# Fewer, larger backward loads, a padded copy of wo in DRAM, and filling products in four 32-column tiles

## The chip, the cores and the metric

One NeuronCore of a Trainium2 chip runs the whole program. The metric is the device time of one execution in microseconds (us); less is better. The engines are named as in the profile: PE (TensorE, matrix products; PEld its weight loads), DVE (VectorE), ACT (ScalarE), POOL (GpSimd) and SP (SyncE, which here only issues transfers). SBUF is the on-chip memory that transfers fill and empty, PSUM the memory that TensorE writes.

## The reference

A transformer block with attention and a gated feed-forward part side by side, and its gradient. 2048 tokens, width 448, 16 heads of 28, feed-forward width 1792, all in bfloat16:

```
xn  = layernorm(x)
q, k, v = split(xn @ wqkv)                      # 16 heads of 28
o   = softmax(q k^T * 28**-0.5) v
out = x + o @ wo + (silu(xn @ w_gate) * (xn @ w_up)) @ w_down
return out, gradients of (x, wqkv, wo, w_gate, w_up, w_down) for grad_out
```

Seven outputs: `out_0` is `out`, `out_1` the gradient of x, `out_2` of wqkv, `out_3` of wo, `out_4` and `out_5` of w_gate and w_up, `out_6` of w_down.

## The kernel before

Heads are taken in four groups of four (G = 4). A head's 28 columns are padded to 32 (HP), so four heads fill the 128 rows of a tile; `pv` rotates the places of the heads by two for V and dO.

**Forward half, 0 to about 611 us.** 256 slots (`slot`), one for each group, block of 512 queries and block of 128 keys, form the scores and their exponentials. Between them a list of units fills TensorE: projections, the feed-forward part with its whole backward (`a_unit`, `u_unit`, `dh_unit`, `dw_unit`), and the attention output with dO (`o_unit`, `mid1` to `mid3`). What the second half needs goes to DRAM: `QD_d` (for each group and query block: Q, dO and both transposed), `KD_d` (K, V, K transposed), `OT_d` (the attention output, transposed), `F_d` (hidden product and its two gradients), `fT_d`, `wT_d`, `wqT_d`.

The output weight wo is loaded once at the start into `wo_pad` (L249-L250): four loads of 28 rows, one for each head of a group, each to rows HP * pv(hh) of a tile that was set to zero (L184). From there DMA transposes fill `woT` (L665), the last of them at slot 13 (L703).

**Backward half, about 614 to 1404 us.** 512 steps k in the order group g, head pair hp, key block kc, query block qc, quarter qi. The loop at L1230 writes out the order of the instructions by hand. Four steps (m = k % 4) make a turn, of which there are 128:

- every step: `row(k)` issues four products in 32-row tiles, two score products of step k into `sb` (L810) and two dO V^T products of step k-1 into `db` (L818). `ew(k)` issues two exponentials on ScalarE (`e_sb`, L834) and two multiplications on VectorE (`ds_sb`, L840), and for three steps of four a DMA transpose of ds (`dst_dma`, L827) on the SP queue. Then SP issues the stores that have waited two steps (`flush`) and the loads that are due (`drop`);
- m = 1: `kv` (dV/dK, L913 and L917: four products in 32-column tiles into `acc`) for the steps that are ready, then `dq_unit` (L944: 16 products in 32-column tiles into `genb`), whose result ScalarE takes away (L948, L957) and POOL adds up (L959);
- m = 2: `kv`, then a filling unit is opened and fills for R2 = 250 ns;
- m = 3: the filling unit goes on for R3 = 750 ns (in one turn of four a `kv` that was put off comes first);
- m = 0: the unit goes on for R0 = 400 ns, the fourth quarter's ds is transposed on TensorE (`tr_unit`, L895, taken away by ScalarE at L900), and the unit is brought to its end.

`fill_step(room)` takes products from the open unit until the room is used up; each `yield` gives a product's estimated ns. With 189 ns a product, R2 takes one and R3 four.

Filling units, in order: `late_dw` (four units of 16 products, the last feed-forward weight gradients), `y_unit` (the forward output: 7 or 11 products for each of 16 token tiles and two halves), `dx_unit` (feed-forward part of the gradient of x: 10, 8 or 10 products, 48 units), `dc_unit` (attention part: 9 products, 16 units), and in between, when a group is done, `dsp_unit` and `dsq_unit` (transposes) and `dwq_unit` (four units of 16 products, gradient of wqkv). A unit's products add up in one bank, `genb`, which has a single buffer shared with `dq_unit`; at its end VectorE or ScalarE takes the bank away. `y_unit` writes `y` (two buffers), which SP stores.

**Loads of the backward half.** `drip(key, pieces, due)` puts pieces of a load into a list ordered by due step. `drop` works through it once a step, at a rate in bytes that meets the due steps (at least 100 KB a step), one SP transfer for each piece (L767). `have(key)` issues at once what is left of a load when it is needed (L773). All transfers of the second half, the transposes among them, go through SP in the order in which they are written. The loads and their pieces: `load_q` (qd, two pieces of 256 KB), `load_k` (kd, 256 and 128 KB), fT (four), wd_sb (seven), wo_sb (four loads of 28 rows from A_wo into a tile that POOL sets to zero, L1048 and L1054), `load_y` (h_c four, x_c two, o_c two for each half), `load_w` (wguT, one for each of 14 blocks), `load_dx` (dau_c, one for each of 14 blocks and four chunks).

The filling products before the change are all of this form (here `dx_unit`), with a weight of 128 columns (64 in the last of four chunks of `late_dw` and `dwq_unit`):

```
PE.matmul(ps[:, :D], lhsT=d[:, i // 2, i % 2, tsl], rhs=dxs["w", fq][:, i // 2, i % 2, :],
          start=(i == 0), stop=(i == n - 1))
```

Of the kernel before, what the change touches and what calls it, by code (L numbers as in the profile page):

```python
# [12 lines left out]
BF16 = mybir.dt.bfloat16  # L13
# [4 lines left out]
D = 448  # L18
H = 16
DH = 28  # L20
# [18 lines left out]
def pv(hh):  # L39


    return (hh + 2) % 4
# [61 lines left out]
def kernel(  # L104
# [32 lines left out]
    OT_d = dram.tile([4, P, G, 512], BF16)  # L137
    F_d = dram.tile([4, P, NFC, 3, 512], BF16)
    fT_d = dram.tile([P, 4, 2, 4, P], BF16)
    wT_d = dram.tile([P, NFC, 2, DP_], BF16)  # L140
    wqT_d = dram.tile([P, 3 * G, DP_], BF16)
    dqkvT_d = dram.tile([3 * G, P, S], BF16)
# [557 lines left out]
    for k in range(12, 16):  # L700
        slot(k)
        if k == 13:
            woT_load(3)  # L703
    qside, kside = {}, {}
    kq = None

# [67 lines left out]

    def load_q(g, qc):
        t = new_q(g, qc)
        drip(("q", g, qc), [(t[:, i:i + 2], QD_d[g, qc, :, i:i + 2]) for i in (0, 2)], 128 * g + 4 * qc - 4)

    def load_k(g, kc):
        t = new_k(g, kc)  # L780
        drip(("k", g, kc), [(t[:, 0:2], KD_d[g, kc, :, 0:2]), (t[:, 2], KD_d[g, kc, :, 2])], 128 * g + 16 * kc - 4)

    steps = [(g, hp, kc, qc, qi) for g in range(G) for hp in range(2) for kc in range(4)
             for qc in range(4) for qi in range(4)]
# [84 lines left out]
        x()  # L869
    fT = bk.tile([P, 4, 2, 4, P], BF16, name="dsp", bufs=1)  # L870
    w2 = bk.tile([P, 4, 2, P], BF16, name="dqT", bufs=1)
    drip(("f",), [(fT[:, sc], fT_d[:, sc]) for sc in range(4)], 10)

    def late_dw(c):
        d0, dn = DCH[c]
        have(("f",))
        ps = ps_g.tile([P, 2, P], FP32, name="genb")
        for t in range(NT):
            PE.matmul(ps[:dn], lhsT=xn_sp[:, t, d0:d0 + dn], rhs=fT[:, t // 4, :, t % 4, :],
                      start=(t == 0), stop=(t == NT - 1))  # L880
            if t < NT - 1:
                yield 110
        DVE.tensor_copy(out=w2[:dn, c], in_=ps[:dn])
        for a, o in enumerate((out_4, out_5)):
            store(o[d0:d0 + dn, F - P:], w2[:dn, c, a])
        yield 110

    dq_acc = bk.tile([P, S // 2], FP32, name="dq_acc", bufs=1)

    def tr_unit(b):  # L890
        for qi in (3,) if b < NB // 4 - 1 else (2, 3):
# [113 lines left out]
    def dwq_unit(g, c, tag="genb"):  # L1005
        d0, dn = DCH[c]
        ps = (ps_b if tag == "rest" else ps_g).tile([P, 3 * P], FP32, name=tag, bufs=2 if tag == "rest" else 1)
        for t in range(NT):
            PE.matmul(ps[:dn, :], lhsT=xn_sp[:, t, d0:d0 + dn], rhs=dsp[g][:, t].rearrange("p k r -> p (k r)"),
                      start=(t == 0), stop=(t == NT - 1))  # L1010
            if t < NT - 1:
                yield 162
        o = bk.tile([P, 3, 4, DH], BF16, name="dwq_o")
        p4 = ps[:].rearrange("p (k h r) -> p k h r", k=3, r=HP)
        cp = ACTE.copy if tag == "rest" else DVE.tensor_copy
        cp(out=o[:dn, 0], in_=p4[:dn, 0, :, :DH])
        cp(out=o[:dn, 1:3, 0:2, :], in_=p4[:dn, 1, :, :DH].rearrange("p (k h) r -> p k h r", k=2))
        cp(out=o[:dn, 2, 2:4, :], in_=p4[:dn, 2, 0:2, :DH])
        cp(out=o[:dn, 1, 2:4, :], in_=p4[:dn, 2, 2:4, :DH])
        store(wq_out[d0:d0 + dn, :, g * 4 * DH:(g + 1) * 4 * DH],  # L1020
              o[:dn].rearrange("p k h r -> p k (h r)"))
        s_done.add((g, c))
        yield 162
# [7 lines left out]
    def load_y(ch, half):  # L1031
        due = now + 32 if now else 36 + 16 * half
        h_c = yp.tile([P, NH, 512], BF16, name="h_c", bufs=3)
        drip(("y", ch, half), [(h_c[:, a:b], F_d[ch, :, half * NH + a:half * NH + b, 0, :])
                               for a, b in ((0, 2), (2, 4), (4, 6), (6, 7))], due)
        ych[ch, half] = h_c
        if half == 0:
            x_c = yp.tile([P, 4, D], BF16, name="x_c")
            drip(("y", ch, half), [(x_c[:, a:a + 2], x_d[:, 4 * ch + a:4 * ch + a + 2, :]) for a in (0, 2)], due)
            ych[ch, 2] = x_c  # L1040
        else:
            o_c = yp.tile([P, G, 512], BF16, name="o_c")
            drip(("y", ch, half), [(o_c[:, a:a + 2], OT_d[ch, :, a:a + 2]) for a in (0, 2)], due)
            ych[ch, 3] = o_c

    wd_sb = yp.tile([P, NFC, D], BF16, name="wd_sb", bufs=1)
    wo_sb = yp.tile([P, G, D], BF16, name="wo_sb", bufs=1)
    POOL.memset(wo_sb[:], 0.0)  # L1048
    wd_v = B_w_down.rearrange("(fc p) d -> p fc d", p=P)
    drip(("y", 0, 0), [(wd_sb[:, a:a + 2, :], wd_v[:, a:a + 2, :]) for a in (0, 2, 4, 6)], 35)  # L1050
    load_y(0, 0)
    load_k(0, 2)
    drip(("y", 0, 1), [(wd_sb[:, a:a + 2, :], wd_v[:, a:a + 2, :]) for a in (8, 10, 12)], 50)
    drip(("y", 0, 1), [(wo_sb[HP * pv(hh):HP * pv(hh) + DH, :, :], wo_v[hh]) for hh in range(4)], 50)  # L1054

    load_y(0, 1)
    load_k(0, 3)
# [1 line left out]
    def y_unit(ch, half, ti):  # L1059
        if ti == 0:  # L1060
            have(("y", ch, half))
            nxt = 2 * ch + half + 2
            if nxt < 8:
                load_y(nxt // 2, nxt % 2)
        tsl = slice(ti * P, (ti + 1) * P)
        mm = [(ych[ch, half][:, i, tsl], wd_sb[:, half * NH + i, :]) for i in range(NH)]
        if half:
            mm += [(ych[ch, 3][:, i, tsl], wo_sb[:, i, :]) for i in range(G)]
        ps = ps_g.tile([P, 512], FP32, name="genb")
        for i, (l, r) in enumerate(mm):  # L1070
            PE.matmul(ps[:, :D], lhsT=l, rhs=r, start=(i == 0), stop=(i == len(mm) - 1))
            if i < len(mm) - 1:
                yield 189
        if half == 0:
            yts[ti] = yp.tile([P, D], FP32, name="yt", bufs=5)
            DVE.tensor_tensor(out=yts[ti][:], in0=ps[:, :D], in1=ych[ch, 2][:, ti, :], op=ALU.add)
        else:
            y = yp.tile([P, D], BF16, name="y")
            DVE.tensor_tensor(out=y[:], in0=ps[:, :D], in1=yts[ti][:], op=ALU.add)  # L1079
            store(out0_d[:, 4 * ch + ti, :], y[:])  # L1080
        yield 189
# [20 lines left out]
    def load_w(fq, due):  # L1102
        f0, f1 = FQ[fq]
        w = dxs["w", fq] = dxs["pool"].tile([P, 5, 2, D], BF16, name="wguT")
        drip(("dx", 0, fq), [(w[:, i - f0], wT_d[:, i, :, :D]) for i in range(f0, f1)], due)

    def load_dx(ch, fq):
        f0, f1 = FQ[fq]
        if ch == 2 and fq < 2:
            load_w(fq + 1, now + 32)  # L1110
        d = dxs["pool"].tile([P, 5, 2, 512], BF16, name="dau_c")
        drip(("dx", ch, fq), [(d[:, i - f0], F_d[ch, :, i, 1:3, :]) for i in range(f0, f1)], now + 16)
        dxs[ch, fq] = d

    def dx_unit(ch, fq, ti):
        if ti == 0:
            have(("dx", ch, fq))
            nxt = 4 * fq + ch + 1
            if nxt < 12:
                load_dx(nxt % 4, nxt // 4)  # L1120
        d = dxs[ch, fq]
        f0, f1 = FQ[fq]
        n = 2 * (f1 - f0)
        tsl = slice(ti * P, (ti + 1) * P)
        ps = ps_g.tile([P, 512], FP32, name="genb")
        for i in range(n):
            PE.matmul(ps[:, :D], lhsT=d[:, i // 2, i % 2, tsl], rhs=dxs["w", fq][:, i // 2, i % 2, :],  # L1127
                      start=(i == 0), stop=(i == n - 1))
            if i < n - 1:
                yield 189  # L1130
        o = dxs["g"][:, 4 * ch + ti, :]
        if fq == 0:
            ACTE.copy(out=o, in_=ps[:, :D])
        else:
            DVE.tensor_tensor(out=o, in0=ps[:, :D], in1=o, op=ALU.add)
        yield 189
# [27 lines left out]
    def dc_unit(t):  # L1164
        if t % 4 == 0:
            have(("dc", t // 4))
            if t < 12:
                load_dc(t // 4 + 1)
        ps = ps_g.tile([P, 512], FP32, name="genb")
        for i in range(3 * G - 3):  # L1170
            PE.matmul(ps[:, :D], lhsT=dcs[t // 4][:, i, (t % 4) * P:(t % 4 + 1) * P], rhs=dxs["wq"][:, i, :],
                      start=(i == 0), stop=(i == 3 * G - 4))
            if i < 3 * G - 4:
                yield 189
        DVE.tensor_tensor(out=dxs["g"][:, t, :], in0=ps[:, :D], in1=dxs["g"][:, t, :], op=ALU.add)
        yield 189
# [53 lines left out]
    for k in range(NB + 12):  # L1230
        now = k
        if k < NB:
# [5 lines left out]
            if hp == 1 and g + 1 < G and qi == 3 and (kc, qc) in NEXT:  # L1238
                load_q(g + 1, NEXT.index((kc, qc)))
        m = k % 4  # L1240
        if k <= NB:
            if k >= K0:
                row(k)
                ew(k)
            flush(k)
            if 2 <= k:
                drop()
# [19 lines left out]
                fill_step(R2)  # L1267
        else:
            fill_step(R3)
    while stream:  # L1270
        for _ in stream.pop(0)[1]():
            pass
# [111 lines left out]
```

The softmax here doesn't subtract the row's maximum and nothing guards it: scores larger than these inputs give would overflow.

## Time and profile before

| | |
|---|---|
| median of 7 runs | 1451.47 us (1447.28 to 1458.43) |
| the profiled execution | 1451.47 us, span of the instructions 1449.7 us |
| PE busy | 1333.7 us (92%), 12647 products |
| ACT busy | 1261.7 us (87%) |
| DVE busy | 1152.4 us (79%) |
| POOL busy | 363.3 us (25%) |
| DMA | 701763 packets, 271.18 MB, mean 187 GB/s |
| mean granted TensorE clock | 0.977 |

Busy time is the union of an engine's instructions. Products on PE are pipelined and their ends are modelled, so the time between the starts of two products tells more than their durations. In the lines of the profile `genb<-wqT,dc 128*128 128x448` is a product into the tile genb of the tiles wqT and dc, with a weight of 128 rows and 128 columns and 448 moving columns; `128*32` is a weight of 32 columns (a column tile), `32*128` one of 32 rows. An arrow in brackets gives idle time before an instruction and what ended it. SP's own lines are issues: their durations are the time that the queue needs to issue a transfer, not that of the transfer.

The costliest groups of the second half are 1024 multiplications on VectorE (L840, 684 ns each), 1024 exponentials on ScalarE (L834, 610 ns), and the four products of each step on TensorE (L810 and L818, L913 and L917).

### The profile page before, as it was taken

The numbers are of one execution on the slowest core, as the hardware profiler recorded it, in microseconds if no ns is written. First come the engines' busy times: TensorE is split into PE (matmuls) and PEld (weight loads), VectorE is DVE, ScalarE is ACT, GpSimd is POOL, SyncE is SP. The second block draws the span as 40 slices with busy tenths as digits, with TensorE's granted clock in tenths as the row PEclk, the third lists the DMA queues.
The fourth block names the chain that finished last, engine by engine and source line by source line (L and its number), as shares of the span: only waits on it lengthen the run. The fifth ranks groups of instructions, "written<-read, shape, count | busy, mean of one in ns | idle before, by whom it ended". The sixth has DMA issues, their size and how long they took to land. (4 is left out here: it accounts for less than half of the span.)

```text
span 1449.7 us, 34726 instructions
## 1 busy us (share of the span) xinstructions
PE 1333.7 (92%) x12647; PEld 542.4 (37%) x12708; DVE 1152.4 (79%) x1997; ACT 1261.7 (87%) x2193; POOL 363.3 (25%) x486
## 2 busy tenths in 40 slices
PE   5899999989999999899898989999999999999996
PEld 2333333333333333333343434433343344444343
DVE  6577757666667666488898989888889999989988
ACT  5799988988989999778898989899889999989974
POOL 6464514453344444010101101101001011010105
PEclk9899999999999999989999999999999999999998
DMA  5797957796778676799999999999999999999971
GB/s 153 164 200 175 223 125 171 173 203 151 169 161 192 134 178 150 194 205 202 225 215 211 214 223 187 214 220 216 222 167 197 202 221 223 205 196 206 195 140 60
DMA packets 701763, 271.18 MB, mean 187 GB/s; under 512 B 620224, under 2 KB 676248, under 8 KB 701592
## 3 DMA queue, kind: packets, MB, share of 16 engines
q1 hardware_dynamic: 696616, 262.83, 88.1%
q0 software_dynamic: 3568, 5.83, 1.9%
q8 instruction: 100, 1.64, 0.5%
q14 instruction: 71, 0.58, 0.1%
q10 hardware_dynamic: 1408, 0.30, 0.1%
HBM read 65.04 MB, written 59.90 MB: 86 GB/s over the span
## 5 line engine op out<-in xcount | busy, mean ns | idle before, releaser
L840 DVE TENSOR_TENSOR ds_sb<-db,e_sb 128x512 bf16<-128x512 f32 x1024 | 646.7, 684 | 54.4 <-issue 22.6
L834 ACT ACTIVATE e_sb<-sb 128x512 bf16<-128x512 f32 x1024 | 554.6, 610 | 65.2 <-PE db L818 48.4
L611 ACT ACTIVATE eT<-s_w 128x1024 bf16<-128x1024 f32 x256 | 263.5, 1029 | 46.0 <-PE s_ps L608 43.1
L613 ACT ACTIVATE eT<-s_ps 128x512 bf16<-128x512 f32 x512 | 279.9, 610 | 0.0
L818 PE MATMUL db<-kd,qd 32*128 32x512 bf16 x1024 | 236.8, 387 | 7.6 <-DVE ds_sb L840 6.8
L810 PE MATMUL sb<-kd,qd 32*128 32x512 bf16 x1024 | 212.0, 391 | 5.6 <-DMA qd<-QD_d 3.8
L959 POOL TENSOR_TENSOR dq_acc<-dq_acc,dq_st 128x256 f32<-128x256 f32 x64 | 46.5, 727 | 570.1 <-ACT dq_st L957 564.4
L917 PE MATMUL acc<-ds_sb,qd 128*32 128x512 bf16 x1024 | 162.2, 394 | 0.0
L913 PE MATMUL acc<-e_sb,qd 128*32 128x512 bf16 x1024 | 160.4, 394 | 1.3 <-DVE dw_o L527 1.3
L900 ACT COPY dsT<-db 128x1024 bf16<-128x1024 bf16 x128 | 130.0, 1016 | 15.8 <-PE db L895 15.1
L379 POOL TENSOR_TENSOR nn<-nn,ag 128x512 f32<-128x512 f32 x56 | 71.3, 1273 | 249.7 <-DVE ag L377 241.1
L608 PE MATMUL s_ps<-QQ,KK 32*128 32x512 bf16 x512 | 126.0, 386 | 4.1
L1127 PE MATMUL genb<-wguT,dau_c 128*128 128x448 bf16 x448 | 117.7, 356 | 6.3 <-ACT dq_st L957 3.9
L608 PE MATMUL s_w<-QQ,KK 32*128 32x512 bf16 x512 | 100.3, 387 | 13.2 <-ACT eT L611 10.5
L810 PEld LDWEIGHTS <-qd 32*128 32x128 bf16 x1024 | 48.3, 91 | 151.6 <-issue 141.8
L420 PE MATMUL gen<-xn_t,f_sp 128*128 128x448 bf16 x416 | 91.8, 354 | 2.6 <-DVE nn L394 1.7
L944 PE MATMUL genb<-dsT,kd 128*32 128x256 bf16 x2048 | 80.4, 278 | 5.5 <-DVE y L1079 3.3
L420 PEld LDWEIGHTS <-f_sp 128*128 128x128 bf16 x640 | 55.7, 98 | 75.0 <-issue 32.0
L895 PE MATMUL db<-ident_bf,ds_sb 128*128 128x128 bf16 x1032 | 80.4, 222 | 0.9 <-DVE ds_sb L840 0.9
L895 PEld LDWEIGHTS <-ds_sb 128*128 128x128 bf16 x1032 | 69.2, 100 | 24.4 <-issue 5.6
L380 POOL TENSOR_TENSOR nn<-nn,tt 128x512 f32<-128x512 f32 x56 | 72.1, 1287 | 4.4
L608 PEld LDWEIGHTS <-KK 32*128 32x128 bf16 x1024 | 29.0, 91 | 115.4 <-issue 111.7
(163 smaller groups left out, 1910.7 us busy)
## 6 DMA issues: line engine op xcount, KB each, us to landing
F_d<-hda SPq DMA_DIRECT2D x56, 384.0 KB
dau_c<-F_d SPq DMA_DIRECT2D x56, 256.0 KB
h_c<-F_d SPq DMA_DIRECT2D x24, 256.0 KB
qd<-QD_d SPq DMA_DIRECT2D x24, 256.0 KB
dsT<-ds_sb SPq DMA_TRANSPOSE x383
dc<-dqkvT_d SPq DMA_DIRECT2D x12, 384.0 KB
wT_d<-wT_f SPq DMA_DIRECT2D x14, 256.0 KB
KD_d<-qk_sp SPq DMA_DIRECT2D x7, 512.0 KB
```

Of the source, the lines that this page charges most:

```text
L420: PE.matmul(ps[:, :D], lhsT=fsp[fc][:, t // 4, w, t % 4, :], rhs=rhs[:, t, :], start=(t == 0), stop=(t == NT - 1))
L608: PE.matmul(sp4[hh], lhsT=KK[g][r:r + HP, kt * P:(kt + 1) * P], rhs=QQ[g][r:r + HP, qsl], start=True, stop=True, tile_position=(r, 0))
L611: ACTE.activation(out=e2[0][:], in_=wide[:], func=ACT.Exp, scale=SCALE)
L613: ACTE.activation(out=e2[1][:, j], in_=sp4[2 + j], func=ACT.Exp, scale=SCALE)
L810: PE.matmul(s_ps[:], lhsT=qside[g, qc][r:r + HP, 0, qi * P:(qi + 1) * P], rhs=kside[g, kc][r:r + HP, 0, :], start=True, stop=True, tile_po ...
L818: PE.matmul(d_ps[:], lhsT=qside[g, qc][r:r + HP, 1, qi * P:(qi + 1) * P], rhs=kside[g, kc][r:r + HP, 1, :], start=True, stop=True, tile_po ...
L834: ACTE.activation(out=est[k][:, j], in_=sps.pop((k, j))[:], func=ACT.Exp, scale=SCALE)
L840: DVE.tensor_tensor(out=ds[:, j], in0=dps.pop((k - 1, j))[:], in1=est[k - 1][:, j], op=ALU.mult)
L895: PE.transpose(ps[:, c, :], ds[:, c // 4, (c % 4) * P:(c % 4 + 1) * P], ident_bf[:])
L900: ACTE.copy(out=o, in_=ps[:])
L913: PE.matmul(a[r:r + HP, :], lhsT=sp4[:, 1, r:r + HP], rhs=e[:, j, :], start=first, stop=last, tile_position=(0, r), skip_group_check=True)
L917: PE.matmul(a[r:r + HP, :], lhsT=sp4[:, 0, r:r + HP], rhs=ds[:, j, :], start=first, stop=last, tile_position=(0, r), skip_group_check=True)
```

## The change

It has three parts.

1. *Loads of the second half in fewer pieces*: qd, kd, x_c and o_c in one piece, fT and h_c in two instead of four, wd_sb in four instead of seven, wguT and dau_c two blocks at a time.
2. *wo padded once*: in slot 13 of the forward half SP stores `wo_pad` (without its last 64 columns) to a new DRAM tile `wo_d`; the second half loads it in one piece of 128 rows, and POOL's memset of `wo_sb` goes.
3. *Filling products in column tiles*: a helper `mm` issues a filling product either as before or, while `split` is set, as four products with 32 columns of the weight each (two where the weight has 64), which write to 32 partitions each of the same bank. The loop sets `split` in the steps m = 2 and m = 3. So a unit's first products are in column tiles, and those of m = 0 in the full array. The transposing units (`dsp_unit`, `dsq_unit`, `tr_unit`) stay as they are, and so does what follows the loop.

```diff
+    wo_d = dram.tile([P, G, D], BF16)
...
         if k == 13:
             woT_load(3)
+            SP.dma_start(out=wo_d[:], in_=wo_pad[:, :, :D])
...
-        drip(("q", g, qc), [(t[:, i:i + 2], QD_d[g, qc, :, i:i + 2]) for i in (0, 2)], 128 * g + 4 * qc - 4)
+        drip(("q", g, qc), [(t[:], QD_d[g, qc])], 128 * g + 4 * qc - 4)
...
-        drip(("k", g, kc), [(t[:, 0:2], KD_d[g, kc, :, 0:2]), (t[:, 2], KD_d[g, kc, :, 2])], 128 * g + 16 * kc - 4)
+        drip(("k", g, kc), [(t[:], KD_d[g, kc])], 128 * g + 16 * kc - 4)
...
-    drip(("f",), [(fT[:, sc], fT_d[:, sc]) for sc in range(4)], 10)
+    drip(("f",), [(fT[:, a:a + 2], fT_d[:, a:a + 2]) for a in (0, 2)], 10)
...
+    split = False
+
+    def mm(ps, lhsT, rhs, start, stop):
+        if not split:
+            PE.matmul(ps, lhsT=lhsT, rhs=rhs, start=start, stop=stop, skip_group_check=True)
+            return
+        for c in range(0, lhsT.shape[1], HP):
+            PE.matmul(ps[c:c + HP], lhsT=lhsT[:, c:c + HP], rhs=rhs, start=start, stop=stop,
+                      tile_position=(0, c), skip_group_check=True)
...
-                               for a, b in ((0, 2), (2, 4), (4, 6), (6, 7))], due)
+                               for a, b in ((0, 4), (4, 7))], due)
...
-            drip(("y", ch, half), [(x_c[:, a:a + 2], x_d[:, 4 * ch + a:4 * ch + a + 2, :]) for a in (0, 2)], due)
+            drip(("y", ch, half), [(x_c[:], x_d[:, 4 * ch:4 * ch + 4, :])], due)
...
-            drip(("y", ch, half), [(o_c[:, a:a + 2], OT_d[ch, :, a:a + 2]) for a in (0, 2)], due)
+            drip(("y", ch, half), [(o_c[:], OT_d[ch])], due)
...
-    POOL.memset(wo_sb[:], 0.0)
...
-    drip(("y", 0, 0), [(wd_sb[:, a:a + 2, :], wd_v[:, a:a + 2, :]) for a in (0, 2, 4, 6)], 35)
+    drip(("y", 0, 0), [(wd_sb[:, a:a + 4, :], wd_v[:, a:a + 4, :]) for a in (0, 4)], 35)
...
-    drip(("y", 0, 1), [(wd_sb[:, a:a + 2, :], wd_v[:, a:a + 2, :]) for a in (8, 10, 12)], 50)
-    drip(("y", 0, 1), [(wo_sb[HP * pv(hh):HP * pv(hh) + DH, :, :], wo_v[hh]) for hh in range(4)], 50)
+    drip(("y", 0, 1), [(wd_sb[:, a:a + 3, :], wd_v[:, a:a + 3, :]) for a in (8, 11)], 50)
+    drip(("y", 0, 1), [(wo_sb[:], wo_d[:])], 50)
...
-        drip(("dx", 0, fq), [(w[:, i - f0], wT_d[:, i, :, :D]) for i in range(f0, f1)], due)
+        drip(("dx", 0, fq), [(w[:, i - f0:min(i + 2, f1) - f0], wT_d[:, i:min(i + 2, f1), :, :D]) for i in range(f0, f1, 2)], due)
...
-        drip(("dx", ch, fq), [(d[:, i - f0], F_d[ch, :, i, 1:3, :]) for i in range(f0, f1)], now + 16)
+        drip(("dx", ch, fq), [(d[:, i - f0:min(i + 2, f1) - f0], F_d[ch, :, i:min(i + 2, f1), 1:3, :]) for i in range(f0, f1, 2)], now + 16)
...
-            PE.matmul(ps[:, :D], lhsT=d[:, i // 2, i % 2, tsl], rhs=dxs["w", fq][:, i // 2, i % 2, :],
-                      start=(i == 0), stop=(i == n - 1))
+            mm(ps[:, :D], d[:, i // 2, i % 2, tsl], dxs["w", fq][:, i // 2, i % 2, :], i == 0, i == n - 1)
...
         m = k % 4
+        split = m > 1
...
+    split = False
     while stream:
```

The products of `late_dw`, `dwq_unit`, `y_unit` and `dc_unit` are replaced by `mm` in the same way.

More of the change, by code (lines that the diff above doesn't have):

```diff
@@ L878, in late_dw @@
         for t in range(NT):
-            PE.matmul(ps[:dn], lhsT=xn_sp[:, t, d0:d0 + dn], rhs=fT[:, t // 4, :, t % 4, :],
-                      start=(t == 0), stop=(t == NT - 1))
+            mm(ps[:dn], xn_sp[:, t, d0:d0 + dn], fT[:, t // 4, :, t % 4, :], t == 0, t == NT - 1)
             if t < NT - 1:
@@ L1008, in dwq_unit @@
         for t in range(NT):
-            PE.matmul(ps[:dn, :], lhsT=xn_sp[:, t, d0:d0 + dn], rhs=dsp[g][:, t].rearrange("p k r -> p (k r)"),
-                      start=(t == 0), stop=(t == NT - 1))
+            mm(ps[:dn, :], xn_sp[:, t, d0:d0 + dn], dsp[g][:, t].rearrange("p k r -> p (k r)"), t == 0, t == NT - 1)
             if t < NT - 1:
@@ L1065, in y_unit @@
         tsl = slice(ti * P, (ti + 1) * P)
-        mm = [(ych[ch, half][:, i, tsl], wd_sb[:, half * NH + i, :]) for i in range(NH)]
+        ops = [(ych[ch, half][:, i, tsl], wd_sb[:, half * NH + i, :]) for i in range(NH)]
         if half:
-            mm += [(ych[ch, 3][:, i, tsl], wo_sb[:, i, :]) for i in range(G)]
+            ops += [(ych[ch, 3][:, i, tsl], wo_sb[:, i, :]) for i in range(G)]
         ps = ps_g.tile([P, 512], FP32, name="genb")
-        for i, (l, r) in enumerate(mm):
-            PE.matmul(ps[:, :D], lhsT=l, rhs=r, start=(i == 0), stop=(i == len(mm) - 1))
-            if i < len(mm) - 1:
+        for i, (l, r) in enumerate(ops):
+            mm(ps[:, :D], l, r, i == 0, i == len(ops) - 1)
+            if i < len(ops) - 1:
                 yield 189
@@ L1170, in dc_unit @@
         for i in range(3 * G - 3):
-            PE.matmul(ps[:, :D], lhsT=dcs[t // 4][:, i, (t % 4) * P:(t % 4 + 1) * P], rhs=dxs["wq"][:, i, :],
-                      start=(i == 0), stop=(i == 3 * G - 4))
+            mm(ps[:, :D], dcs[t // 4][:, i, (t % 4) * P:(t % 4 + 1) * P], dxs["wq"][:, i, :], i == 0, i == 3 * G - 4)
             if i < 3 * G - 4:
```

## The prediction

> **What bounds the kernel now.** I read the table of stretches first, then the waits of the same stretches, then the SP queue and VectorE in order of time around the longest wait, then TensorE in one ordinary turn. The backward loop is a chain of 128 turns of four steps (k % 4 = 0 to 3; m below), from about 614 us to 1404 us. The columns of the stretches are busy time of each engine, then the granted clock, the DMA share and GB/s.
>
> ```profile
> 660.00:760.00 100.00, 91.65 (x1027) 36.55 (x1025) 87.76 (x144) 88.66 (x165) 8.71 (x12) 0.97 1.08 216
> 760.00:860.00 100.00, 91.22 (x1035) 38.20 (x1033) 86.88 (x142) 86.15 (x160) 8.72 (x12) 0.95 1.11 215
> 1100.00:1200.00 100.00, 96.67 (x1118) 39.73 (x1115) 95.16 (x156) 93.85 (x176) 9.45 (x13) 1.00 1.07 211
> 1300.00:1400.00 100.00, 97.34 (x1123) 39.52 (x1120) 96.35 (x162) 92.90 (x172) 6.81 (x10) 1.00 1.00 184
> ```
>
> From 1100 us on, three engines are busy 93 to 97%; from 660 to 860 us all three are busy 86 to 92%, so nobody's work is the bound there. The waits from 660 to 860 us (total, times, longest) tell what they wait for:
>
> ```profile
> DVE ds_sb L840 <- DMA dsT<-ds_sb: 5.1, 4, 2.2
> DVE y L1079 <- DMA out_dram<-y: 4.5, 2, 2.8
> PE genb L944 <- DVE y L1079: 3.3, 2, 2.3
> PEld L1071 <- DMA o_c<-OT_d: 1.5, 1, 1.5
> ```
>
> VectorE waits for buffers that a transfer has still to read, TensorE for VectorE or for a load. From 860 to 1400 us the only wait for a transfer in the thirty largest is one of 5.7 us on POOL. The longest of these waits, on VectorE and on the SP queue:
>
> ```profile
> 760.74 0.62 DVE L1079 TENSOR_TENSOR y<-genb,yt 128x448 bf16<-128x448 f32 x1 [0.29 <-PE genb L1071]
> ...
> 775.55 0.62 DVE L1079 TENSOR_TENSOR y<-genb,yt 128x448 bf16<-128x448 f32 x1 [2.79 <-DMA out_dram<-y]
> ```
>
> ```profile
> 769.17 3.98 SPq L827 DMA_TRANSPOSE dsT<-ds_sb  x2
> 773.20 0.57 SPq L800 DMA_DIRECT2D out_dram<-y  x1
> 773.87 1.23 SPq L827 DMA_TRANSPOSE dsT<-ds_sb  x1
> 775.15 0.57 SPq L767 DMA_DIRECT2D h_c<-F_d  x1
> 775.82 1.23 SPq L827 DMA_TRANSPOSE dsT<-ds_sb  x1
> 777.11 0.58 SPq L767 DMA_DIRECT2D h_c<-F_d  x1
> ```
>
> `y` has two buffers, so the addition at 775.55 needs the store of the one made at 760.74, which ended at 761.36. That store is issued at 773.20, 11.8 us later. The program holds it two steps back, some 2.9 us; the other 9 us are queue. SP issues without a pause: 1.29 us from a transpose's start to the next issue (775.82 to 777.11), 0.67 us for a direct transfer (775.15 to 775.82). From 660 to 860 us the issue list counts 95 transposes and 94 direct transfers: 95 x 1.29 + 94 x 0.67 = 185.5 us of 200. **The SP queue's issue time is the bound of that stretch**, and a late store, transpose or load is what the others meet.
>
> What it costs: TensorE's dQ products (L944) begin a turn; four ordinary turns, 1334.33 to 1357.53, take 23.20 us, 5.80 each (so do the four from 783.50 to 806.71). From 674.37 to 858.24 us there are 29 turns in 183.87 us, 15.7 us more than 29 x 5.80 = 168.2. About 2.5 us of that are turns with longer filling, so some 13 us come with the waits (10.5 us of waits on VectorE and TensorE, then the slow clock and recovery behind them).
>
> **The loads.** Of the loads that SP issues at L767 (and, on demand, at L773) the change takes out 88: fT 2, wd_sb 3, wo_sb 3, h_c 16, x_c 4, o_c 4, qd 12, kd 14, wguT 6, dau_c 24. It adds one store of 448 KB. Bytes are the same, so the transfers' own time is taken as unchanged. An issue's price hardly goes with its size: in the queue's timeline a dc load of 384 KB takes 0.59 us, a kd third of 128 KB 0.58 us. From 660 to 860 us it removes h_c 14, x_c 4, o_c 4, qd 4, kd 3, wo_sb 3, wd_sb 1: 33 x 0.67 = 22 us, and seven more (5 us) from 611 to 660 us. SP's demand falls from 185 to 163 us of 200; the backlog of 9 us is gone within the first 80 us. I take 10 us of the 13 as gained, because one wait is for a load that is fetched when its unit begins (o_c, 1.5 us) and can stay in part; bounds 0 and 13. After 860 us 48 issues go as well: 0 us, as no wait there ends with a transfer on the path; what hides them is ScalarE's and VectorE's work on the scores (without that cover, 48 x 0.67 = 32 us).
>
> What becomes later: a 512 KB load occupies the rings 2.4 us at the 215 GB/s of the table instead of 1.2 us, so what is issued behind it (a transpose, a y store) lands up to 1.2 us later. Before, the store issued at 773.20 to 773.77 released VectorE at 775.55, 1.8 us after its issue. I take nothing for it, since 1.2 us is small against 9 us of backlog saved; the rival below prices it.
>
> **wo through DRAM.** The store of the padded wo comes on SP behind the last transpose of wo, 64.48 to 65.74; SP's next transpose starts at 66.81, as it waits for a POOL load (to 66.69). The 0.67 us fit into that 1.0 us: 0 us, at most +0.7 without this cover, for the forward transposes queued behind it. The POOL memset that goes (1.61 us at 625.5) lay beside everything; POOL is busy 9% of each stretch above: 0.
>
> **Products in four column tiles.** One ordinary turn on TensorE:
>
> ```profile
> 1351.68 0.61 PE L944 MATMUL genb<-dsT,kd 128*32 128x256 bf16 x16
> 1352.23 0.39 PE L810 MATMUL sb<-kd,qd 32*128 32x512 bf16 x2
> ...
> 1352.78 0.38 PE L913 MATMUL acc<-e_sb,qd 128*32 128x512 bf16 x2
> 1352.79 0.38 PE L917 MATMUL acc<-ds_sb,qd 128*32 128x512 bf16 x2
> 1353.10 0.36 PE L1171 MATMUL genb<-wqT,dc 128*128 128x448 bf16 x1
> 1353.40 0.39 PE L810 MATMUL sb<-kd,qd 32*128 32x512 bf16 x2
> 1353.40 0.48 PE L818 MATMUL db<-kd,qd 32*128 32x512 bf16 x2
> 1353.82 0.93 PE L1171 MATMUL genb<-wqT,dc 128*128 128x448 bf16 x4
> ```
>
> Four products of 512 columns in four column tiles follow each other at 0.22 us. From the last group (1352.78) to the filling product (1353.10) it is 0.32 us, from that product to the rows 0.30 us, where 448 columns alone take 0.19 us: a change of tiling costs 0.10 us. With the filling product in the dV/dK tiling the first change goes, the second stays. 112 turns have such a product behind dV/dK: 112 x 0.10 = 11 us if all lay on the path. But the rows at m = 3 already wait: the db group of 1353.40 takes 0.48 us instead of 0.39, because its last product needs a buffer that VectorE still reads. A TensorE that arrives 0.10 us earlier there waits 0.10 us longer. That more TensorE work is free also shows in the turns: with 7 fillers (783.50 on) and with 9 (1334.33 on) four turns take the same 23.2 us. The gain is left to the 16 turns with 16 long fillers (6.4 to 6.7 us each), 1.6 us; I take -1.5, bounds 0 and -11.
>
> Of the split products only one in five stands behind dV/dK; the other four, at m = 3, follow the score rows and save nothing. 96 turns of 1 + 4, 12 of 2 + 5 and 4 of 2 + 7 make 600 split products, some 1,740 more products and as many weight loads. Their price is from the nearest row, L944: 16 tiled products of 256 columns with 16 loads in 0.55 us (1351.68 to 1352.23, a tiling change of 0.10 in it) is 0.11 us for a group of four, 256 columns' own time, so loads and issue are hidden and 448 columns hide them better. Entering column tiles from the rows takes about 0.01 us more than entering the full array (over all turns the median time beyond the rows' 512 columns is 0.101 us before L913, 0.090 us before the fillers at m = 3): 112 x 0.01, +1. Lower bound 0; upper bound, if four tiles ran one after another, 3 x 0.19 us x 600 = 340 us, far from that row.
>
> [...]
>
> **Sum.** The profiled execution took 1451.47 us (span 1449.7, 1.8 around it) and is the median of the seven runs. 1451.5 - 10 (SP) - 1.5 (tiling change) + 1 (entry at m = 3) = **1441 us**.
>
> **Rivals.** *The rings, not SP, are the bound.* For it: DMA share 1.08 to 1.11 in the stretch. Against: 1.07 at 1100 to 1200 us without such waits, and the store above landed within 1.8 us of its issue. Then only tiling is gained: 1451.5 - 0.5 to - 2 = 1450 us. *Both pay in full*: 1451.5 - 13 - 11 = 1427 us; against it the 0.48 us row. *Slower: bigger loads stop the transposes.* In the y stretch some 37 loads double; if half of them hold a transpose or store 1.2 us past the moment its buffer is needed, 18 x 1.2 = +22 us, and with no relief 1473 us, with it 1463. It decides once the remaining backlog plus landing exceeds the ten ds_sb buffers' lead (ten steps, 14.5 us; with 9 us of backlog it was just exceeded four times). *Slower: split products cost more than L944 says*: each 0.1 us dearer gives 600 x 0.1 = 60 us, less some 0.2 us of slack in each of 112 turns (22 us): 1479 us. *The change doesn't do what it says*: four fifths of the split products have no dV/dK in front; that is in the sum.
>
> **How the numbers follow.** SP relief with little from tiling, 1434 to 1447 us: 0.58. Both in full: 0.10. Rings: 0.15. Bigger loads slower: 0.12. Dear split products: 0.05. About 0.3% (4.4 us) is what a measurement can tell from no change. Faster (below 1447.1): 0.58 + 0.10 and a little of the rings = 0.70. Same: 0.15. Slower: 0.15. The range 1431 to 1454 leaves out most of the second case and of the two slow ones, 2 in 10.
>
> **What would show it.** Right: from 660 to 860 us no wait of VectorE for out_dram or dsT, VectorE above 93% there, the 29 turns near 170 us, and the store of a y issued within 5 us of it. Tiling: no 0.10 us before the filling product at m = 2, the last db product at m = 3 waiting longer instead, turns of 5.80 us unchanged from 1300 us on. Wrong: turns above 5.9 us from 1300 us on (split products cost), or the same waits with SP issuing less (rings).

## The result, and the profile after

The change does nothing that can be measured. The changed kernel takes 1451.54 us (median of 27 runs, 1447.72 to 1459.35), the kernel before 1451.54 us beside it (median of 64 runs); the ratio is 1.0006 with a 95% interval of 0.9997 to 1.0016. The profiled execution took 1451.77 us, span 1450.0 us. The stated range, 1431 to 1454, holds the time, but the forecast was 1441 us, and its largest term is not there.

The stretches of the changed kernel, with the columns of the table before (busy time of PE, PEld, DVE, ACT, POOL, then granted clock, DMA share, GB/s):

```profile
660.00:760.00 100.00, 90.50 (x1148) 37.28 (x1145) 84.46 (x138) 85.20 (x159) 8.73 (x12) 0.91 1.14 209
760.00:860.00 100.00, 91.77 (x1262) 39.45 (x1260) 88.95 (x146) 88.45 (x165) 8.74 (x12) 0.98 1.15 218
1100.00:1200.00 100.00, 96.10 (x1358) 41.01 (x1355) 95.33 (x155) 93.78 (x178) 9.94 (x14) 1.00 1.11 209
1300.00:1400.00 100.00, 97.34 (x1374) 41.31 (x1376) 96.33 (x163) 92.29 (x173) 6.84 (x10) 1.00 1.09 190
```

The hole from 660 to 860 us is as deep as before: VectorE 84 and 89% there against 95 and 96% later. The waits of that stretch have not gone either (total, times, longest):

```profile
DVE y L1088 <- DMA out_dram<-y: 7.4, 2, 3.9
...
PE genb L955 <- DVE y L1088: 6.2, 2, 3.2
...
DVE ds_sb L842 <- DMA dsT<-ds_sb: 3.9, 5, 1.8
```

VectorE's two waits for transfers come to 11.3 us, where they were 9.6. The 29 turns that took 183.9 us before take 184.6 (678.56 to 863.13); the prediction wanted some 170.

SP's queue in order of time around the longest wait, with the issues of several transposes in a row drawn together:

```profile
700.88 7.22 SPq L829 DMA_TRANSPOSE dsT<-ds_sb  x4
708.15 0.58 SPq L769 DMA_DIRECT2D h_c<-F_d  x1
708.82 1.23 SPq L829 DMA_TRANSPOSE dsT<-ds_sb  x1
710.14 0.57 SPq L802 DMA_DIRECT2D dqkvT_d<-dkv  x1
710.82 5.58 SPq L829 DMA_TRANSPOSE dsT<-ds_sb  x3
716.45 0.57 SPq L769 DMA_DIRECT2D h_c<-F_d  x1
717.15 2.83 SPq L829 DMA_TRANSPOSE dsT<-ds_sb  x2
720.03 1.50 SPq L802 DMA_DIRECT2D out_dram<-y  x1
```

and the additions into y on VectorE:

```profile
709.13 0.62 DVE L1088 TENSOR_TENSOR y<-genb,yt 128x448 bf16<-128x448 f32 x1 [0.29 <-PE genb L895]
714.95 0.62 DVE L1088 TENSOR_TENSOR y<-genb,yt 128x448 bf16<-128x448 f32 x1 [0.29 <-PE genb L895]
724.53 0.62 DVE L1088 TENSOR_TENSOR y<-genb,yt 128x448 bf16<-128x448 f32 x1 [3.90 <-DMA out_dram<-y]
```

There are fewer direct transfers between the transposes, as the change meant. But SP still issues without a pause, because a transpose takes longer: four in 7.22 us are 1.80 us each and three in 5.58 are 1.86 (the short gaps between them included), where a lone one behind a direct transfer takes 1.23. The y made at 709.13 is stored at 720.03, 10.3 us after it was ready; before it was 11.8. Then its buffer comes free later: VectorE goes on 4.50 us after the issue of that store began (720.03 to 724.53), where it was 2.35 us before (773.20 to 775.55). Over the stretch, counted from SP's own lines:

| 660 to 860 us | transposes, mean us to issue | direct transfers, mean us | sum of SP's issues |
|---|---|---|---|
| before | 94, 1.35 | 94, 0.61 | 183.8 us |
| after | 94, 1.57 | 59, 0.68 | 187.1 us |

What the direct transfers gave back, 57.1 - 39.9 = 17 us, the 94 transposes took: 147.2 - 126.7 = 20.5 us. The rise is not even. The first transpose behind a direct transfer takes 1.36 us in the mean (1.37 before); the second in a row takes 1.92 (1.29 before).

The sum of the issues doesn't tell the hole from the rest: from 1100 to 1200 us, where nothing waits for a transfer on the path, SP's issues take 91.4 of 100 us before and 91.9 after. What differs there is how late they come. A transpose is issued 1.2 us (after the change 1.5) behind the multiplication on VectorE that made its ds; from 660 to 860 us it is 7.5 us, and 6.3 after the change.

The tiling did what it says. One ordinary turn on TensorE after the change:

```profile
1354.69 0.38 PE L928 MATMUL acc<-ds_sb,qd 128*32 128x512 bf16 x2
1354.90 0.36 PE L898 MATMUL genb<-wqT,dc 128*32 128x448 bf16 x4
1355.20 0.39 PE L812 MATMUL sb<-kd,qd 32*128 32x512 bf16 x2
1355.21 0.58 PE L820 MATMUL db<-kd,qd 32*128 32x512 bf16 x2
1355.72 0.94 PE L898 MATMUL genb<-wqT,dc 128*32 128x448 bf16 x16
```

From the last dV/dK group to the filling product it is 0.21 us now, 0.31 before: the change of tiling is gone. The rows behind it show where the 0.10 us went: the db group takes 0.58 us instead of 0.48, since its last product waits for the same buffer. Four split products take 0.94 us, the four whole ones took 0.93. Four ordinary turns take 23.12 us (1330.47 to 1353.59), 23.20 before.

### The profile page after: what moved, and what is told of

The parts are those of the page before. It is cut to its first block, busy times and chain, and to the rows that moved or that the text cites. A ratio compares the mean times of both kernels' runs of the same rounds, so it can differ in the third digit from the quotient of the medians.

```text
span 1450.0 us, 38114 instructions
## 1 busy us (share of the span) xinstructions
PE 1331.4 (92%) x14387; PEld 554.0 (38%) x14448; DVE 1152.8 (80%) x1997; ACT 1259.6 (87%) x2193; POOL 361.8 (25%) x485
## 5 line engine op out<-in xcount | busy, mean ns | idle before, releaser
L820 PE MATMUL db<-kd,qd 32*128 32x512 bf16 x1024 | 241.5, 388 | 8.8 <-DVE ds_sb L842 7.8
L955 PEld LDWEIGHTS <-kd 128*32 128x32 bf16 x2048 | 55.6, 98 | 42.6 <-issue 15.6
```

The source lines that it names most:

```text
L820: PE.matmul(d_ps[:], lhsT=qside[g, qc][r:r + HP, 1, qi * P:(qi + 1) * P], rhs=kside[g, kc][r:r + HP, 1, :], start=True, stop=True, tile_po ...
L955: PE.matmul(ps[r:r + HP, :256], lhsT=ks[:, kt, h:h + HP], rhs=t[:, par::2, j, kt, :], start=(kt == 0), stop=(kt == 3), tile_position=(0, r ...
```

## The experiments

Ratios are to runs of the kernel before on the same chip, in five rounds each, 95% interval in brackets; 0.1% is 1.45 us. A kernel's "29 turns" are the same 29 turns as above in its own profile.

### Each half of the change alone

The merged loads alone are the changed kernel with

```diff
-        split = m > 1
+        split = False
```

> The changed kernel with split always off: parts 1 and 2 of the change alone. Theory SP (the queue's issue time is the bound from 660 to 860 us, as the prediction has it, and the split products gave the gain back): ratio to the kernel before 0.993 (-10 us), no wait of VectorE for out_dram or dsT. Theory rings (the transfers' own time is the bound, so fewer issues gain nothing): ratio 0.998 to 1.002, the waits of VectorE for transfers from 660 to 860 us stay near 10 us in sum, and SP's transposes take longer to issue than 1.35 us in the mean.

Measured: 1453.85 us, ratio 1.0005 [0.9986, 1.0023]. VectorE waits 6.5 us for the store of y and 3.1 us for dsT; the 29 turns take 183.8 us; a transpose takes 1.60 us to issue. So the loads alone do nothing, and no gain of theirs is hidden by a loss of the tiles.

The tiles alone are the kernel before with `mm` and `split`.

> The kernel before with the split products alone (part 3). Theory SP with a costly split: ratio 1.005 or more (+8 us), DMA share above that of before in every stretch. Theory rings: ratio 0.997 to 1.000: one 0.10 us of tiling change less in every fourth turn and in the turns with 16 long fillers, 2 to 4 us after 860 us, nothing before.

Measured: 1454.13 us, ratio 1.0014 [0.9998, 1.0031]; the waits are there as before (7.3 us for dsT, 6.3 for y). The interval runs from 0.3 us faster to 4.5 us slower, so a gain of the tiles can't be told from nothing.

### More issues

In the kernel before, every late load of 128 rows goes as two halves of 64 rows:

```diff
-        slow.extend((due, key, o, i) for o, i in pieces)
+        for o, i in pieces:
+            if o.shape[0] == P:
+                slow.extend((due, key, o[h:h + 64], i[h:h + 64]) for h in (0, 64))
+            else:
+                slow.append((due, key, o, i))
```

> The kernel before with every load of 128 rows in the backward half issued as two of 64 rows each: the same packets and bytes, some 52 more issues from 660 to 860 us. Theory SP: 52 x 0.67 = 35 us more issue time in a stretch where SP has 15 us left, so +20 us or more, ratio above 1.013. Theory rings: the queue has only been waiting for the rings, and the ratio stays below 1.004.

Measured: 1560.26 us, ratio 1.074 [1.0712, 1.0768], 107 us more, far above either figure. The stretches:

```profile
660.00:760.00 100.00, 83.13 (x765) 29.61 (x763) 66.98 (x107) 68.45 (x124) 8.71 (x12) 0.81 0.94 173
760.00:860.00 100.00, 86.56 (x926) 34.40 (x923) 79.69 (x130) 80.24 (x148) 7.25 (x10) 0.93 0.98 179
```

The transfer engines move less (share 0.94 and 0.98, GB/s down to 173 and 179), a transpose takes no longer to issue than before (1.33 us in the mean, 1.35 before), and yet VectorE waits longest for transposes:

```profile
DVE ds_sb L844 <- DMA dsT<-ds_sb: 21.0, 16, 3.0
```

So here the number of issues sets the pace. From 600 us on SP issues 514 direct transfers where the kernel before has 315: 107 us / 199 = 0.54 us for each added one, near the issue time of 0.57; the slower clock (0.81 and 0.93) is in that figure. The prediction's queue is real on this side, and all through the second half: the 84 turns behind the first 36 take 574.9 us instead of 510.4.

### Fewer bytes, with the issues left and with the issues cut

The first kernel is the one before with its small loads; of the second half's h_c it fetches 16 columns of 512 for chunks 1 to 3, in as many pieces:

```diff
-        h_c = yp.tile([P, NH, 512], BF16, name="h_c", bufs=3)
+        n = 512 if ch == 0 else 16
+        h_c = yp.tile([P, NH, n], BF16, name=f"h_c{half}" if ch == 0 else "h_n", bufs=1 if ch == 0 else 3)
...
-        ych[ch, half] = h_c
+        ych[ch, half] = h_c if ch == 0 else ych[0, half]
```

> The kernel before, in which y_unit multiplies the h_c of chunk 0 for all four chunks, and the h_c loads of chunks 1 to 3 are issued as before but fetch 16 columns of 512 (5.2 MB less from 660 to 860 us; out_0 is not the reference's there). Theory SP: as many issues, so the waits stay: ratio 0.998 to 1.002. Theory rings: some 12% fewer bytes in that stretch, most waits for out_dram and dsT gone: ratio 0.995 or below (-8 us).

Measured: 1455.21 us, ratio 1.0021 [1.0007, 1.0035]. 5.3 MB less (262.8 to 257.5 MB on SP's queue) gain nothing either; 7.8 us of waits for the store of y are left. It is not a clean test of bytes alone: `drop` counts bytes, so the four narrow pieces of a half go out in a row, where the wide ones stood between transposes.

Then the same cut of bytes with the merged loads (without tiles):

> The merged loads without the tiles, with as many issues as in the run of the merged loads alone, but the h_c loads of chunks 1 to 3 fetch 16 of 512 columns (5.3 MB less); the units of y take chunk 0's h_c throughout, so y is computed from chunk 0's h. It parts the two reliefs that stood together in the run with both. Theory of two limits (with the issues already cut, what is left is what the rings move): most of the 9 us comes with the bytes alone, 1443 to 1448, DVE's waits for DMA in 660 to 860 under 5 us. Theory of issues (the twelve further issues did it): 1450 to 1454, waits of 8 us or more, as with the merged loads alone.

Measured: 1446.84 us, ratio 0.9961 [0.9946, 0.9976], 5.7 us less; the 29 turns take 178.8 us. VectorE's waits for transfers are 6.5 us, where under 5 were expected. And with those h_c loads left out altogether, twelve issues fewer again:

> The merged loads without the tiles, and of h_c only chunk 0 is loaded; the units of y for chunks 1 to 3 take it again, so that y is computed from chunk 0's h in all four chunks. The queue of SP loses twelve more issues and the rings some 2.8 MB of 272. Theory of two limits (SP's issue time and what the rings can move stand close together there, and relief of either alone leaves the other): with both relieved a transpose is back at some 1.3 us of issue in 660 to 860 us, SP's lag behind ds_sb falls under 4 us after the first 60 us, DVE's waits there fall from 11 us to under 4, and the time is 1441 to 1446. Theory of the prediction (issue time alone) says the same and can't be told apart here. Theory of order (the waits come from the second y buffer and from the place of the stores in the queue, not from how much passes through it): DVE still waits 4 to 8 us for the store of y, and the time is 1449 to 1454.

(The bytes in this expectation are wrong: six halves of 0.92 MB are 5.5 MB.) Measured: 1444.14 us, ratio 0.9935 [0.9912, 0.9959], 9.4 us less. Its stretches and waits:

```profile
660.00:760.00 100.00, 90.23 (x1027) 36.65 (x1026) 88.99 (x146) 89.93 (x168) 8.70 (x12) 1.00 1.13 203
760.00:860.00 100.00, 94.48 (x1112) 40.00 (x1109) 93.64 (x153) 92.62 (x172) 9.44 (x13) 1.00 1.09 202
```

```profile
DVE y L1089 <- DMA out_dram<-y: 2.8, 2, 2.0
PE genb L955 <- DVE y L1089: 1.6, 2, 1.2
DVE ds_sb L842 <- DMA dsT<-ds_sb: 0.9, 3, 0.5
```

Here is the picture that was predicted for the change: VectorE at 94% in the second hundred, 3.7 us of waits, 29 turns in 177.3 us, and close to the 10 us. It came with fewer issues and fewer bytes together. The theory of two limits had the time right in both; the theory of issues fails on the kernel with the narrow loads, which has as many issues as the merged loads alone. What both runs take away are the halves of h_c, which the merged loads fetch in pieces of 512 and 384 KB, so that fewer bytes and fewer large loads are not told apart. Two details missed: a transpose still took 1.54 us to issue, not 1.3, and SP's lag behind ds_sb, mostly under 4 us from 731 us on, went above it again (up to 6.3 us) between 812 and 845 us.

### Fewer and larger still

Each half of h_c, each group of wguT and each dau_c in one load (changed kernel without tiles), as in

```diff
-                               for a, b in ((0, 4), (4, 7))], due)
+                               for a, b in ((0, 7),)], due)
```

> The changed kernel without the tiles, and with each half of h_c, each group of wguT and each dau_c in one load in place of two or three: some 38 issues fewer again (8 of them before 900 us), the bytes the same. Theory of issues (SP's issue time is the bound): 8 times 0.57 us less for SP in 660 to 860, the lag falls and the time is 1445 to 1449. Theory of two limits: with the bytes as before nothing is won, 1450 to 1455; SP's issues still fill over 180 of the 200 us because a transpose takes 1.6 us or more to issue.

Measured: 1455.54 us, ratio 1.0026 [1.0010, 1.0043], some 4 us slower, with 194 direct issues in the second half against 228. SP's issues fill 186.4 of 200 us with a transpose at 1.64. The issues theory fails again, this time with the wrong sign.

### A deeper buffer for y

The changed kernel with four buffers:

```diff
-            y = yp.tile([P, D], BF16, name="y")
+            y = yp.tile([P, D], BF16, name="y", bufs=4)
```

> The changed kernel with four buffers of y in place of two; nothing else. Theory of order: the waits of DVE for the store of y (7.4 us in 660 to 860) are gone, nothing takes their place, and the time is 1443 to 1447. Theory of two limits: the queue of SP stays as full, so the wait moves to ds_sb or to dsT, DVE's waits for DMA in 660 to 860 stay at 8 us or more, and the time is 1449 to 1453.

Measured: 1455.55 us, ratio 1.0014 [0.9994, 1.0033]. The wait for the store of y is gone from the list and another has grown in its place, on ds_sb for dsT: 9.3 us, where it was 3.9. So the place of the wait was not the cause here.

### Loads or stores through POOL

The changed kernel with the late loads (`drop` and `have`) issued by POOL:

```diff
-            SP.dma_start(out=o, in_=i)
+            POOL.dma_start(out=o, in_=i)
```

> The changed kernel with the late loads of the backward part issued by POOL in place of SP; the bytes are the same. Theory of the prediction (SP's issue time is the bound from 660 to 860 us): SP has only the transposes and stores left, its lag falls under 3 us, the waits of DVE for out_dram and dsT are gone, and the time is 1440 to 1446. Theory of the rings (what the 16 engines can move sets how fast the transposes pass): SP's issues still take some 185 of 200 us or the transposes land as late as before, waits of 8 us or more stay, and the time is 1448 to 1454. POOL's adds of dq_acc then wait behind its issues; if that decides, the time is over 1455 and PE waits for genb.

Measured: 1497.41 us, ratio 1.0324 [1.0279, 1.0370]. POOL now waits in front of loads whose buffers are not free yet; its waits from 660 to 1400 us:

```profile
POOL dc L769 <- PE genb L895: 26.6, 1, 26.6
POOL h_c L769 <- PE genb L895: 23.4, 1, 23.4
POOL dau_c L769 <- PE genb L895: 22.8, 2, 14.0
```

The run is spoiled as a test of SP's time alone by these, but not as a test of what SP's transposes meet: with 26 direct transfers left on SP from 660 to 860 us, a transpose takes 1.91 us to issue, where it takes 1.57 in the changed kernel with 59. The price is not set by SP's neighbours in its queue alone: with the loads on another queue it rose.

Then only the stores (`flush`) by POOL, in the changed kernel, in the kernel before, and with the merged loads without tiles:

```diff
             _, o, i = held.pop(0)
-            SP.dma_start(out=o, in_=i)
+            POOL.dma_start(out=o, in_=i)
```

> The changed kernel with the stores of the backward part (y, dw, dqkvT and the like) issued by POOL in place of SP; the loads stay on SP and the bytes are the same. Theory of two limits: the transposes take the time that the stores leave, SP's issues still fill over 180 of 200 us in 660 to 860, DVE waits for dsT in place of out_dram, 1449 to 1455. Theory of issues and order (y's store no longer stands behind late transposes and SP has some 26 issues less there): the waits for out_dram and dsT together fall under 4 us and the time is 1441 to 1446.

> The kernel before with its stores of the backward part issued by POOL in place of SP and nothing of the change in it: the loads stay small and the products whole. If SP's issues and the rings' load are near-equal limits, taking 26 stores in 200 us off SP and its ring relieves both at once, and this gives about what the same move gave in the changed kernel, 1443 to 1448, with the waits for out_dram gone. If the move pays only where the loads are merged (the issue time had to fall first, and POOL's stores free the ring), this stays at 1449 to 1453 and waits of 8 us for dsT remain.

> The merged loads and POOL's stores without the tiles. Beside the changed kernel with POOL's stores it shows what the column tiles are worth where the queue stalls less, beside the kernel before with POOL's stores what the merged loads are worth there. From the turns of the profiles (every fourth 0.10 us shorter with the tiles, the next 0.02 longer) the tiles are worth 1.5 to 3.5 us: 1446 to 1450 here. If the tiles are worth nothing, 1444 to 1446.

| stores by POOL, with | median | ratio | 29 turns |
|---|---|---|---|
| the whole change | 1445.48 us | 0.9961 [0.9941, 0.9980] | 181.2 us |
| nothing of the change | 1445.34 us | 0.9941 [0.9916, 0.9967] | 178.1 us |
| merged loads, no tiles | 1444.49 us | 0.9954 [0.9932, 0.9975] | 175.7 us |

All three are faster than the kernel before, by 6 to 9 us, and the intervals overlap: with the stores out of SP's way neither the merged loads nor the tiles add anything that can be told. The first expectation came out mixed: the time of the theory of issues and order, with the wait for dsT (7.2 us) and SP's full queue (189.9 of 200 us) of the other. The second came out as the first of its two cases, the third as tiles that are worth nothing. The kernel before with POOL's stores:

```profile
660.00:760.00 100.00, 94.79 (x1061) 38.15 (x1060) 89.40 (x146) 90.69 (x170) 14.61 (x23) 0.94 1.15 224
760.00:860.00 100.00, 92.06 (x1051) 39.39 (x1054) 89.76 (x146) 88.25 (x165) 15.89 (x26) 0.97 1.13 222
```

```profile
DVE ds_sb L840 <- DMA dsT<-ds_sb: 0.5, 1, 0.5
```

With the small loads a transpose takes 1.42 us to issue, 98 of them pass in the 200 us where 94 did, and all the data pass that the kernel before passes. In that stretch the engines move 224 and 222 GB/s, where they move 216 and 215 in the kernel before: those were not the most that they can move here.

### The same bytes on one queue and on the other

Into the kernel before with POOL's stores come six loads that nobody reads, one more copy of each late half of h_c (5.5 MB), once issued by POOL, once through SP's list:

```diff
         ych[ch, half] = h_c
+        if ch:
+            POOL.dma_start(out=scr[:], in_=F_d[ch, :, half * NH:half * NH + NH, 0, :])
```

> The kernel before with POOL's stores, and six more loads that nobody reads: each half of h_c of chunks 1 to 3 (0.92 MB) is fetched once more into a scratch tile, issued by POOL. SP's queue is as in the run with POOL's stores, the 16 engines move 5.5 MB more in some 250 us. Theory of the queue (what counts is what passes through SP's own queue, issues and bytes): no change from that run, 1443 to 1448. Theory of the engines (all queues share what the engines can move, and they are full): 5.5 MB at 220 GB/s are 25 us of their time, the waits for dsT come back and the time is 1452 to 1470.

> The same six extra loads, but on SP's queue beside the real h_c loads (six issues more, 5.5 MB more). Theory of the queue: the relief that POOL's stores gave is used up, 1451 to 1458, while the run with the same bytes on POOL stays under 1448. Theory of the engines: about the same time as with the bytes on POOL.

Measured: 1462.81 us, ratio 1.0073 [1.0058, 1.0089] by POOL, 1459.50 us, ratio 1.0055 [1.0036, 1.0075] by SP. Against the same kernel without them (0.9941) that is 1.3% and 1.1%, 19 and 17 us; the 29 turns take 198.9 and 192.7 us, 178.1 without them. By POOL:

```profile
660.00:760.00 100.00, 87.13 (x933) 34.09 (x931) 80.12 (x131) 80.70 (x150) 17.98 (x26) 0.93 1.13 223
760.00:860.00 100.00, 90.62 (x961) 36.95 (x960) 82.33 (x134) 81.89 (x153) 17.68 (x27) 0.93 1.13 228
```

```profile
DVE ds_sb L840 <- DMA dsT<-ds_sb: 12.2, 7, 3.7
```

SP's queue is free of these bytes, and yet the transposes are late and VectorE waits 12.2 us for them. The theory of the queue fails; what delays SP's transposes is shared by the queues of SP and POOL. (By SP the list names only 1.2 us of waits for dsT; what holds VectorE there was not found.) Whether the stores on POOL gained issue time and nothing else, no run here shows.

The added loads are also far larger than the others of these kernels, 896 KB in one piece. On SP the transposes behind one of them, up to the next direct transfer, take 3.76 us over their 1.23 each, those behind an h_c load of 256 KB 0.32: 3.5 times the bytes, twelve times the delay. The same bytes in small pieces were not run, so these two runs don't tell the sum of the bytes from the size of a piece.

## Why the prediction was wrong

**The step that failed** is the 10 us of "The loads": "SP's demand falls from 185 to 163 us of 200; the backlog of 9 us is gone within the first 80 us." It took 1.29 us a transpose as a fixed price and moved only the number of direct transfers. The price is not fixed: it went from 1.35 to 1.57 us as the loads got larger (1.60 with the merged loads alone, 1.64 with loads merged further), the demand came to 187 us (183.8 before), and the backlog stayed but for some 1 us (6.3 us behind ds_sb, 7.5 before). Measured, the term is 0 us. A line that the prediction shows spoke against a fixed price: the two transposes from 769.17 take 3.98 us.

**"I take nothing for it"**, said of what is issued behind a larger load, is the same mistake from the other end. The delay came twice. In the issue: the transposes between an h_c load and the next direct transfer took 0.18 us over their 1.23 before and 0.66 after, those behind a qd load 0.23 and 1.34 (sums from SP's lines, per load). And in the landing: in each kernel VectorE waits for two stores of y between 660 and 860 us. Before the change it went on 2.40 and 2.35 us after their issue began, with it 4.50 and 3.84 us after. The rival "bigger loads stop the transposes" had this mechanism; its price, 12 to 22 us above the kernel before, did not come.

**"The SP queue's issue time is the bound of that stretch"** was half right. Adding issues costs 0.54 us apiece at once. Taking 35 away by merging loads gives nothing, taking 26 away by moving the stores gives 6 to 9 us, so it is not the number alone. Something that the queues of SP and POOL share counts as well: adding 5.5 MB costs 17 to 19 us on either. Whether that is the sum of the bytes or the size of single loads is not shown. Nor was the fullness of SP's queue a sign of the bound: its issues sum to 183 to 190 us of 200 in the slow kernels and in the fast ones. Of the rivals, "the rings, not SP, are the bound" named the time (1450) and the sign by which to know it (the same waits, with SP issuing less); its reason is as one-sided as the forecast's. The argument used against it, that the same DMA share stands at 1100 to 1200 us without waits, was no evidence: that share was 1.07 there before and is 1.11 after, with no wait in either.

**The tiling terms** (-1.5 and +1) held as far as can be seen. The place of the 0.10 us, the longer wait of the db group and the free split products are as foretold; the dear split products of the rival, 1479 us, did not come. Four ordinary turns gain 0.08 us, 2 us if all 112 do; the four long turns of one `dwq_unit` group take 25.85 us instead of 26.31, 1.8 us if all four groups do. In the times nothing of this is seen: tiles alone 1.0014, and with POOL's stores 0.9961 with tiles against 0.9954 without.

**wo through DRAM** held at 0: its store takes SP from 65.16 to 65.76 us and the next transpose starts at 66.75, 66.81 before.

**What stays open**: why 26 stores moved from SP to POOL gained 6 to 9 us with the bytes unchanged, while 35 direct transfers fewer by merging loads gained nothing. It fits that the moved stores leave the loads small (a transpose at 1.42 us instead of 1.60), but with merged loads and POOL's stores a transpose took 1.70 us and the gain was there all the same. What a transpose's issue waits for was not seen directly, only that it is longer where larger loads are under way. It does not go by the bytes moved in the stretch: 1.35 us at 215 GB/s before, 1.57 at 213 after, 1.42 at 223 with the stores of the kernel before on POOL.

## What to carry to other kernels

When a queue issues without a pause, don't read its issue times as fixed prices: they can grow with what else is under way (here a transpose's from 1.35 to 1.57 us), and then issues saved are eaten by the ones that remain (17 us by 20.5). Test both sides first, a run with more issues and one with larger or added loads; if both cost time at once, a merge that trades the one for the other has little to gain (here 0 us). The gains here came with issues taken off the queue while the loads stayed as they were (the moved stores, 6 to 9 us), or with large loads taken out (9.4 us). The cheap move here was to take what is never urgent, the stores, to an engine that has time (POOL, busy 14.6 and 15.9 of 100 us with the stores on it), and to leave on the old queue the loads that wait for buffers (one held POOL for 26.6 us).

## What the runs showed of the hardware

- Halving loads by rows cost 107 us for 199 more issues, with the bytes the same; from 660 to 860 us the transfer engines moved 173 and 179 GB/s, where they moved 216 and 215 before.
- In the changed kernel a stop of TensorE was followed by a slower clock: it is idle for 3.18 us up to 725.21, and the granted clock of the next 10 us is 0.66, 1.00 before:

```profile
725.21 0.62 PE L955 MATMUL genb<-dsT,kd 128*32 128x256 bf16 x16 [3.18 <-DVE y L1088]
```

```profile
715.00:725.00 10.00, 7.03 (x98) 2.80 (x95) 5.97 (x10) 7.53 (x14) 0.73 (x1) 1.00 1.20 200
725.00:735.00 10.00, 9.35 (x104) 4.62 (x103) 8.42 (x15) 6.56 (x13) 1.40 (x2) 0.66 1.07 242
```

  ScalarE is busy for 6.56 of 10 us behind it, 7.53 in the 10 us before. In the kernel before, a stop of 2.35 us up to 776.23 is followed by 0.59 from 777 to 781 us. The run with four y buffers shows 0.66 from 740 to 750 us too, and the longest wait of TensorE in its list from 660 to 860 us is 2.1 us. Not every stop was followed by it: in the changed kernel TensorE is idle for 1.46 us up to 694.00, and the clock from 700 to 710 us is 1.00. What decides was not measured.
